# Attention's places in the cycles, loads of a unit one by one, word loads ahead of stores, prologue copies on two engines

## The chip, the core and the metric

The program runs on one core of a Trainium2 chip. The metric is the device time of one execution in microseconds (us); the number for a kernel is the median of its runs. The core has a matrix engine (PE, TensorE), a vector engine (DVE), a scalar engine (ACT), GpSimd (POOL) and a sequencer that mostly asks for transfers (SP). All run beside each other, each takes its own instructions strictly in program order, and they wait for one another through semaphores.

## What is computed

Attention without a score matrix, for 8 batches, 8 heads, 576 positions, 64 columns per head; then two MLPs (512 to 2048 to 512) over all 4608 tokens:

```python
q_s = softmax of q over its 64 columns
k_s = softmax of k over the 576 positions
kv  = einsum('bhsd,bhse->bhde', k_s, v)
x   = einsum('bhsd,bhde->bhse', q_s, kv)          # then (4608, 512)
h = x @ w_in;  x = (h * sigmoid(h)) @ w_out                      # MLP 0
h = x @ w_in2; out = (h * clip(h + 3, 0, 6) / 6) @ w_out2        # MLP 1
```

All inputs are float32; the weights come as 64-bit words, which the kernel turns into float32 on the chip.

## The kernel before

**Cycles.** The tokens are cut into nine tiles of 512: tile t is the first 512 positions of batch t, and tile 8 gathers the 64 positions that each batch has left over (`rest`). The hidden width is cut into eight pairs of 128-column blocks. A cycle g does one MLP m, one tile t and one pair p (`place`, L556), so there are 2 x 9 x 8 = 144 cycles. Cycles 0 to 7 (`first_cycle`, L777) multiply plainly in float32. Cycles 8 to 143 (`cycle`, L687) form the first product of the MLP by a seven-product scheme: `product` (L564) takes one seventh of the tile `ring`, which holds prepared weights, and each operand is split into a high and a low part, so that three matmuls (`mm3`, L72 to L75) stand for one. Two ring buffers take turns, and `load_w` (L264) asks for the ring of cycle g + 2 as soon as cycle g has done its last product. The sum out of PSUM called `s2` (L745) must be done before the seventh product may overwrite its bank B; L750 and L755 are the two sums behind it. `bend` (L579) applies the activation, and `layer_out` (L601, also called G) does the second matmuls one cycle later.

**Ticks.** A cycle has eight places called ticks, `side(0)` to `side(7)`. `run(8 * g + k)` (L683) issues whatever the table `events` holds for that tick. A unit u is one pair of heads of one batch: 32 units. Units 0 to 3 are done in the prologue (L833 to L893), units 4 to 7 in cycles 0 to 7, and the other 24 (`turned`, L275) in cycles 8 to 55, one per two cycles. The loop at L659 gives each unit u a tick x at which its output is formed, and each step a place before it, such as `(-4, at_tsplit)`. So cycles come in two sorts: in one PE forms `kv` of a unit, in the next its output x.

**A unit's steps** (L281 to L496). `at_load` asks for the unit's data: k and the turned q in one tile `kq`, q by rows, and a tile `ev` with k by rows and v. `at_soft` finds the maxima of k (`nm`) and q (`qm`) on DVE and shifts q on GpSimd. `at_sendnm` and `at_send` write such columns to DRAM (`nmd`, `qm`, `qr`), `at_shift` and `at_spread` read them back spread over many partitions (`nb`, `qm`, `qr`). GpSimd then adds (`at_tadd` L330, `at_sub` L382) and multiplies (`at_tmul` L338), ACT takes exponents (`at_texp`, `at_exp`), `at_norm` (L395) forms the reciprocal sums of q on DVE, and `at_tsplit` (L340) splits the turned q into `qh` (ACT) and `ql` (DVE). All these transfers are asked for on SP.

**Weights of MLP 1.** In cycles 56 to about 80 the words of MLP 1 are converted beside the products. `feed` (L84) asks for words into `st` on ACT's queue, `converting` (L114) turns them into `w` (ACT: `magnitude`, L122; DVE: L125 to L140), `operands_w` (L172) forms the seven operands `r`, and `keep` (L203) stores `r` to DRAM, also on ACT's queue. `chain` (L249) strings the jobs of `second` (L231) together, and `pump` (L104) issues their steps by a budget per tick. The weights of MLP 0 go the same way in cycles 0 to 7 (`convert_in`, `convert_out`, L156 to L166).

The order of the instructions on each engine is the order in which this program is written; the framework adds only the waits.

Of the kernel before, what the change touches and what calls it, by code (L numbers as in the profile page):

```python
# [8 lines left out]
F32 = mybir.dt.float32  # L9
# [8 lines left out]
P = 128  # L18
# [17 lines left out]
def attention_two_mlps(ctx: ExitStack, tc: tile.TileContext, kqT, kv5, qn, w1, w2, out):  # L36
# [212 lines left out]
    def chain(jobs, second_mlp=False):  # L249

        out = []
        for k, j in enumerate(jobs):
            if k and len(jobs[k - 1]) < 10:
                out += j[:1]
                j = j[1:]
            elif k:
                out[-1:-1] = j[:1]
                j = j[1:]
            if k and second_mlp and len(jobs[k - 1]) >= 10:
                j = j[:1] + [(0, feed)] + j[1:]  # L260
            out += j
        return out

# [8 lines left out]
    def ahead(u):  # L272
        return u < NP

    def turned(u):  # L275
        return u >= TURNED * NP
# [4 lines left out]
    def at_load(u):  # L281
        b, c = divmod(u, NP)
        s = un[u] = {}
        if ahead(u):
            s["k"] = pro_p.tile([P, S], F32, tag="k", name="k")
            nc.sync.dma_start(out=s["k"], in_=kqT[b, c, :, :S])
        elif turned(u):
            kq = ld_p.tile([P, 2, S], F32, tag="k", name="kq")
            nc.sync.dma_start(out=kq.rearrange("p a s -> p (a s)"), in_=kqT[b, c])
            s["k"], s["t"] = kq[:, 0], kq[:, 1]  # L290
        else:
            s["k"] = ld_p.tile([P, 2, S], F32, tag="k", name="k")[:, 0]
            nc.sync.dma_start(out=s["k"], in_=kqT[b, c, :, :S])
        p = pro_p if ahead(u) else ld_p
        s["q"] = p.tile([QP, 2 * QJ, D], F32, tag="q", name="q")
        nc.sync.dma_start(out=s["q"].rearrange("p j d -> p (j d)"), in_=qn[b, c])
        if ahead(u):
            s["e"] = p.tile([P, 5, P], F32, tag="e", name="e")
            return
        ev = p.tile([P, 2, 5, P], F32, tag="ev", name="ev")  # L300
        s["e"], s["v"] = ev[:, 0], ev[:, 1]
        if turned(u):
            nc.sync.dma_start(out=ev.rearrange("p a j d -> p (a j d)"), in_=kv5[b, c])
        else:
            nc.sync.dma_start(out=s["v"].rearrange("p j d -> p (j d)"), in_=kv5[b, c, :, 5 * P:])

    def at_load_v(u):
        b, c = divmod(u, NP)
# [28 lines left out]
        s = un[u]  # L337
        nc.gpsimd.tensor_tensor(out=s["t"], in0=s["t"], in1=s["qr"], op=ALU.mult)  # L338

    def at_tsplit(u):  # L340
        s = un[u]
        s["qT"] = (
            at_p.tile([P, S], F32R, tag="qh", name="qh"),
            at_p.tile([P, S], F32R, tag="ql", name="ql"),
        )
        split(*s["qT"], s["t"])

    def at_soft(u):
        s = un[u]
# [71 lines left out]
    def at_trq(u, i):  # L421
        s = un[u]
        q = s["q"]
        bq = bank("tq")
        for j in range(3):
            nc.tensor.transpose(
                bq[:, j * QP:(j + 1) * QP],
                q[:, (3 * i + j) * 2:(3 * i + j) * 2 + 2, :].rearrange("p j d -> p (j d)"),
                ident[:QP, :QP],
            )  # L430
        if i == 0:
            if plain(u):
                s["qT"] = at_p.tile([P, S], F32, tag="qh", name="qf")
            else:
                s["qT"] = (
                    at_p.tile([P, S], F32R, tag="qh", name="qh"),
                    at_p.tile([P, S], F32R, tag="ql", name="ql"),
                )
        sl = slice(i * 288, (i + 1) * 288)
        if plain(u):  # L440
            nc.scalar.copy(s["qT"][:, sl], bq[:, :288])
        else:
            qh, ql = s["qT"]
            split(qh[:, sl], ql[:, sl], bq[:, :288])
# [35 lines left out]
    def at_xhalf(u, i):  # L480
        b, c = divmod(u, NP)
        s = un[u]
        bx = bank("x")
        sl = slice(0, HT) if i == 0 else slice(HT, S)
        n = sl.stop - sl.start
        if plain(u):
            nc.tensor.matmul(bx[:, :n], lhsT=s["kv"], rhs=s["qT"][:, sl], start=True, stop=True)
        else:
            (kh, kl), (qh, ql) = s["kv"], s["qT"]
            mm3(bx[:, :n], kh, kl, qh[:, sl], ql[:, sl], True, True)  # L490
        if b == 0:
            nc.scalar.copy(first_x(c)[:, i * HT:(i + 1) * HT], bx[:, :HT])
        else:
            nc.scalar.copy(x_raw(b)[:, c, i * HT:(i + 1) * HT], bx[:, :HT])
        if i:
            nc.scalar.copy(rest[:, c, b * 64:(b + 1) * 64], bx[:, HT:n])  # L496

# [127 lines left out]
    def put(m, t, c, y):  # L625
        if c == 0:
            ys[m, t] = y_p.tile([P, KC, DM], F32, tag="y", name="y")
        o = ys[m, t]
        scale = 0.5 if m == 0 else 1.0
        if c % 2:  # L630
            nc.scalar.activation(out=o[:, c], in_=y, func=AF.Copy, scale=scale)
        else:
            nc.vector.tensor_scalar_mul(o[:, c], y, scale)
        if m and t == NB - 1:
            rows = out.rearrange("(b s) d -> b s d", b=B)[2 * c:2 * c + 2, TB:, :]
            nc.sync.dma_start(out=rows, in_=o[:, c])
# [11 lines left out]
    events = {}  # L648
    m2_p = []
    pre = []  # L650

    def at(tick, fn, *args):
        events.setdefault(tick, []).append((fn, args))
# [4 lines left out]

    for u in range(NP, NU):  # L659
        x = x_at(u)  # L660
        at(x_at(u - 2) - 5 if u - 2 >= NP else -90, at_load, u)
        if turned(u):
            plan = [
                (-28, at_soft), (-27, at_kexp), (-26, at_sendnm), (-26, at_send, "qm"), (-25, at_qexp),
                (-24, at_knorm), (-23, at_norm), (-21, at_shift), (-21, at_spread, "qm"),
                (-20, at_send, "qr"), (-15, at_spread, "qr"), (-14, at_tadd), (-13, at_sub),
                (-10, at_texp), (-9, at_exp), (-8, at_tmul), (-4, at_tsplit),
            ]
        else:
            plan = [  # L670
                (-18, at_soft), (-17, at_kexp), (-16, at_qexp), (-14, at_trk, 0), (-14, at_knorm), (-13, at_norm),
                (-12, at_trk, 1), (-9, at_trq, 0), (-8, at_trq, 1),
            ]
        plan += [(-6, at_kv), (-4, at_kvsplit), (0, at_xhalf, 0), (2, at_xhalf, 1)]
        for d, fn, *args in plan:
            at(x + d, fn, u, *args)
# [100 lines left out]
    def first_cycle(g):  # L777
        A, B_ = banks["A"], banks["B"]

        def side(k):  # L780
            run(8 * g + k)
            pump(FIRST, keep=True)
            if g == NC - 1:
                if k in (2, 3):
                    sums_x(1, k - 2)
                for i in {3: (5,), 4: (1, 6), 5: (2, 3), 6: (7, 4)}.get(k, ()):
                    operand_x(1, i)

        def G(k):
            if g:  # L790
                layer_out(g - 1, k)

        pre = prepare_in(g - 1) if 0 < g < NC - 1 else []
        words_in = convert_in(g + 1) if g + 1 < NC else []
        if g == 1:
            steps.extend(words_in + convert_out(g) + pre)
        else:
            steps.extend(pre[:4] + words_in + pre[4:] + convert_out(g))
# [24 lines left out]
        side(6)  # L823
        G(7)
        side(7)

    with tc.manual_schedule():
# [71 lines left out]
            banks[k] = main_ps.tile([P, TB], F32, tag=k, name=k)  # L899
        for tick in sorted(k for k in events if -90 < k < 0):  # L900
            run(tick)
        for p in range(NC):
            first_cycle(p)
            pump(99)
# [56 lines left out]
```

## Time and profile before

| | |
|---|---|
| median of 3 runs | 1744.61 us (1743.39 to 1744.97) |
| the profiled execution | 1744.62 us, span of its instructions 1742.8 us |
| PE busy | 1655.8 us, 95% of the span |
| DVE, ACT, GpSimd busy | 1034.8 (59%), 739.3 (42%), 182.6 us (10%) |
| moved by DMA | 399.01 MB, mean 229 GB/s |
| granted TensorE clock | 0.988 of full speed |

The span is the time between the first and the last instruction that the profiler saw. A busy share of the whole span is an average over stages with different limits, so the rows below take the stages apart; in the rows by stretch a number in brackets counts instructions, the clock is the granted share of TensorE's full clock, and the DMA column is the mean busy share of the 16 DMA engines. "Idle before" in a row is the time for which that engine did nothing before the instruction, and the arrow names what ended it.

### The profile page before, as it was taken

To read this page: it belongs to the slowest core of one execution; us is meant where nothing else is said; L and a number is where in the kernel's file an instruction comes from. 1 tells how busy PE (TensorE), PEld (TensorE's weight loads), DVE (VectorE), ACT (ScalarE), POOL (GpSimd) and SP (SyncE) were. 2 spreads that over 40 slices of the span, in tenths; PEclk is the share of its full clock that TensorE was granted. 3 is DMA by queue.
4 is the path that set the end of the run, shared out by engine and by line. 5 is a ranking of instruction groups with operands and counts; after the bars stand their busy time and mean duration, and the time that the engine had idled before them with its cause. 6 is when DMAs were issued, how large, how long until landed. Compare 5 with 4: busy or idle time off the path is not lost.

```text
span 1742.8 us, 25018 instructions
## 1 busy us (share of the span) xinstructions
PE 1655.8 (95%) x9816; PEld 1422.0 (82%) x9816; DVE 1034.8 (59%) x1733; ACT 739.3 (42%) x1396; POOL 182.6 (10%) x124
## 2 busy tenths in 40 slices
PE   7899999999999999999999899999999999999994
PEld 4444888888888887898888789999999999999993
DVE  6889677475655657467868674535353535353531
ACT  5444555444443545344545343434343434343431
POOL 2211222231222223200000000000000000000000
PEclk9999999999999999999999999999999999999997
DMA  8568969989998899868887755464655555555540
GB/s 298 189 224 269 259 222 245 234 271 223 239 267 258 235 237 263 226 234 315 328 312 299 305 193 218 169 225 182 230 179 218 192 195 197 202 206 207 197 169 24
DMA packets 71037, 399.01 MB, mean 229 GB/s; under 512 B 20232, under 2 KB 23304, under 8 KB 45320
## 3 DMA queue, kind: packets, MB, share of 16 engines
q1 hardware_dynamic: 66312, 351.27, 63.7%
q10 hardware_dynamic: 4608, 46.14, 6.8%
q8 instruction: 78, 1.28, 0.3%
q14 instruction: 39, 0.32, 0.1%
HBM read 348.91 MB, written 48.47 MB: 228 GB/s over the span
## 4 chain that ended last, share of the span: by engine, by line
PE 70%; DMA 15%; DVE 9%; ACT 2%; issue 1%; POOL 1%; SPq 1%; ACTq 0%; POOLq 0%; DVEq 0%
PE y L73 12%; PE y L74 11%; PE y L75 11%; PE B L73 5%; PE B L74 5%; PE B L75 5%; PE A L73 4%; PE A L74 4%; PE A L75 4%; DMA ring<-wd 4%; DMA qr<-qr 4%; DMA st<-w_dram 3%; DMA q<-qn_dram 2%; PE C L75 2%; PE C L74 2%; PE C L73 2%
## 5 line engine op out<-in xcount | busy, mean ns | idle before, releaser
L70 DVE TENSOR_TENSOR gs<-g,gs 128x512 fp32r<-128x512 f32 x272 | 202.0, 743 | 157.9 <-ACT gs L69 156.4
L73 PE MATMUL B<-o,ring 128*128 128x256 f32 x816 | 234.5, 287 | 30.7 <-DVE s L745 19.9
L69 ACT CAST gs<-g 128x512 fp32r<-128x512 f32 x272 | 168.5, 620 | 207.3 <-DVE g L591 207.0
L73 PE MATMUL A<-op,ring 128*128 128x256 f32 x816 | 231.5, 284 | 10.5 <-DMA ring<-wd 8.6
L74 PE MATMUL A<-op,ring 128*128 128x256 f32 x816 | 230.8, 283 | 1.0 <-DVE op L70 0.9
L75 PE MATMUL B<-o,ring 128*128 128x256 f32 x816 | 231.0, 283 | 0.0
L74 PE MATMUL B<-o,ring 128*128 128x256 f32 x816 | 230.9, 283 | 0.0
L75 PE MATMUL A<-op,ring 128*128 128x256 f32 x816 | 230.8, 283 | 0.0
L73 PE MATMUL y<-woh,gs 128*128 128x512 f32 x576 | 227.8, 395 | 0.0
L74 PE MATMUL y<-wol,gs 128*128 128x512 f32 x576 | 227.7, 395 | 0.0
L75 PE MATMUL y<-woh,gs 128*128 128x512 f32 x576 | 224.5, 390 | 0.0
L73 PEld LDWEIGHTS B<-o,ring 128*128 128x128 f32 x816 | 155.2, 190 | 63.3 <-DVE s L745 29.3
L73 PE MATMUL y<-gs,woh 128*128 128x512 f32 x512 | 205.8, 402 | 0.0
L74 PE MATMUL y<-gs,woh 128*128 128x512 f32 x512 | 203.6, 398 | 0.0
L75 PE MATMUL y<-gs,wol 128*128 128x512 f32 x512 | 201.0, 393 | 0.0
L73 PEld LDWEIGHTS A<-op,ring 128*128 128x128 f32 x816 | 155.9, 191 | 20.6 <-issue 5.0
L74 PEld LDWEIGHTS B<-o,ring 128*128 128x128 f32 x816 | 155.0, 190 | 15.4 <-issue 0.5
L74 PEld LDWEIGHTS A<-op,ring 128*128 128x128 f32 x816 | 155.9, 191 | 6.8 <-DVE op L70 1.4
L75 PEld LDWEIGHTS A<-op,ring 128*128 128x128 f32 x816 | 155.9, 191 | 0.0
L75 PEld LDWEIGHTS B<-o,ring 128*128 128x128 f32 x816 | 155.0, 190 | 0.0
L589 ACT ACTIVATE g<-A,half 128x512 f32<-128x512 f32 x72 | 49.6, 688 | 245.6 <-DVE A L750 245.6
L745 DVE TENSOR_TENSOR s<-B,s 128x256 f32<-128x256 f32 x136 | 57.4, 422 | 158.5 <-PE B L75 156.2
(155 smaller groups left out, 2981.5 us busy)
## 6 DMA issues: line engine op xcount, KB each, us to landing
ring<-wd SPq DMA_DIRECT2D x134, 1792.0 KB, 8.0
st<-w_dram SPq DMA_DIRECT2D x16, 1024.0 KB, 8.3
st<-w_dram ACTq DMA_DIRECT2D x16, 1024.0 KB, 10.6
ev<-kv_dram SPq DMA_DIRECT2D x24, 640.0 KB, 9.8
wd<-ring ACTq DMA_DIRECT2D x8, 1792.0 KB, 9.6
wd<-r ACTq DMA_DIRECT2D x8, 1792.0 KB, 7.6
kq<-kqT_dram SPq DMA_DIRECT2D x24, 576.0 KB, 8.0
q<-qn_dram SPq DMA_DIRECT2D x32, 288.0 KB, 8.5
```

The costliest lines, as they stand in the source:

```text
L69: nc.scalar.copy(hi, src)
L70: nc.vector.tensor_tensor(out=lo, in0=src, in1=f32(hi), op=ALU.subtract)
L73: nc.tensor.matmul(o, lhsT=wh, rhs=xh, start=start, stop=False, **kw)
L74: nc.tensor.matmul(o, lhsT=wh, rhs=xl, start=False, stop=False, **kw)
L75: nc.tensor.matmul(o, lhsT=wl, rhs=xh, start=False, stop=stop, **kw)
L589: nc.scalar.activation(out=a, in_=hb, func=AF.Relu, scale=1.0 / 6.0, bias=half)
L745: nc.vector.tensor_tensor(out=s2, in0=B_[:, lo], in1=s5, op=ALU.add)
```

## The change

1. In a unit of cycles 8 to 55, k, q, `ev` and the turned q (now a tile `t` of its own) are asked for one by one at places of their own; the order on SP changes.
2. The unit's later steps move: `at_tadd`, `at_sub` to tick 0 of a cycle, `at_tmul` from -8 to -4, `at_norm` from -23 to -20, `at_tsplit` is cut into `at_tcast` (ACT) at -3 and `at_tlow` (DVE) at -1. The steps of units 4 to 7 move by one place here and there.
3. In `chain`, the store of a job comes behind the next job's word load.
4. In the first cycles, the `magnitude` of the next weights comes one step earlier in the list.
5. In the prologue, the second half of each PSUM copy goes to DVE.
6. Two of the last four output stores are asked for on ACT's queue.

```diff
@@ chain
             if k and second_mlp and len(jobs[k - 1]) >= 10:
-                j = j[:1] + [(0, feed)] + j[1:]
+                j = j[:1] + [(0, feed), store] + j[1:]
+            if second_mlp and len(jobs[k]) >= 10:
+                store = j[-1]
+                j = j[:-1]
@@ at_load (turned units: kq in one, ev behind it), now at_load, at_load_ev, at_load_t
-            kq = ld_p.tile([P, 2, S], F32, tag="k", name="kq")
-            nc.sync.dma_start(out=kq.rearrange("p a s -> p (a s)"), in_=kqT[b, c])
-            s["k"], s["t"] = kq[:, 0], kq[:, 1]
+        s["k"] = p.tile([P, S], F32, tag="k", name="k")
+        nc.sync.dma_start(out=s["k"], in_=kqT[b, c, :, :S])
...
+    def at_load_t(u):
+        b, c = divmod(u, NP)
+        un[u]["t"] = t = ld_p.tile([P, S], F32, tag="t", name="t")
+        nc.sync.dma_start(out=t, in_=kqT[b, c, :, S:])
@@ at_tsplit
-    def at_tsplit(u):
+    def at_tcast(u):
...
-        split(*s["qT"], s["t"])
+        nc.scalar.copy(s["qT"][0], s["t"])
+
+    def at_tlow(u):
+        s = un[u]
+        nc.vector.tensor_tensor(out=s["qT"][1], in0=s["t"], in1=f32(s["qT"][0]), op=ALU.subtract)
@@ at_trq, at_xhalf
-            nc.scalar.copy(s["qT"][:, sl], bq[:, :288])
+            (nc.vector.tensor_copy if ahead(u) and i else nc.scalar.copy)(s["qT"][:, sl], bq[:, :288])
...
+        copy = nc.vector.tensor_copy if ahead(u) and i else nc.scalar.copy
+        copy((x_raw(b)[:, c] if b else first_x(c))[:, i * HT:(i + 1) * HT], bx[:, :HT])
         if i:
-            nc.scalar.copy(rest[:, c, b * 64:(b + 1) * 64], bx[:, HT:n])
+            copy(rest[:, c, b * 64:(b + 1) * 64], bx[:, HT:n])
@@ put
-            nc.sync.dma_start(out=rows, in_=o[:, c])
+            (nc.scalar if c % 2 else nc.sync).dma_start(out=rows, in_=o[:, c])
@@ the places
-        at(x_at(u - 2) - 5 if u - 2 >= NP else -90, at_load, u)
+        elif turned(u):
+            at(max(x - 42, 0 if turned(u - 2) else before - 11), at_load, u)
+            at(x - 36, at_load_ev, u)
+            at(x - 32, at_load_t, u)
...
-                (-24, at_knorm), (-23, at_norm), (-21, at_shift), (-21, at_spread, "qm"),
-                (-20, at_send, "qr"), (-15, at_spread, "qr"), (-14, at_tadd), (-13, at_sub),
-                (-10, at_texp), (-9, at_exp), (-8, at_tmul), (-4, at_tsplit),
+                (-21, at_shift), (-21, at_spread, "qm"), (-20, at_knorm), (-20, at_norm), (-18, at_send, "qr"),
+                (-12, at_tadd), (-12, at_sub), (-11, at_spread, "qr"), (-10, at_texp), (-9, at_exp),
+                (-4, at_tmul), (-3, at_tcast), (-1, at_tlow),
...
-                (-18, at_soft), (-17, at_kexp), (-16, at_qexp), (-14, at_trk, 0), (-14, at_knorm), (-13, at_norm),
-                (-12, at_trk, 1), (-9, at_trq, 0), (-8, at_trq, 1),
+                (-18, at_soft), (-17, at_kexp), (-15, at_qexp), (-14, at_trk, 0), (-13, at_knorm), (-13, at_norm),
+                (-12, at_trk, 1), (-8, at_trq, 0), (-7, at_trq, 1),
@@ first_cycle (coming holds the jobs whose magnitude is already in the list)
-        words_in = convert_in(g + 1) if g + 1 < NC else []
+        o = convert_out(g)
+        if g + 1 < NC:
+            i = coming.pop()
+            i[-1:-1] = o[:1]
+            if g + 2 < NC:
+                coming.append(convert_in(g + 2))
+                o[-1:-1] = [coming[0].pop(0)]
+            o = o[1:]
```

SP's queue over one unit of cycles 8 to 55, in the kernel before (`nb`, `nmd`, `qm`, `qr` are the columns that go through DRAM, `ring` the prepared weights):

```order
L267 DMA ring<-wd 128x3584
L326 DMA qr<-qr 64x576 x2
L372 DMA nmd<-nm 128x1
L317 DMA qm<-qm 96x2x6
L267 DMA ring<-wd 128x3584
L377 DMA nb<-nmd 128x128
L326 DMA qm<-qm 64x576 x2
L289 DMA kq<-kqT_dram 128x1152
L296 DMA q<-qn_dram 96x768
L303 DMA ev<-kv_dram 128x1280
L317 DMA qr<-qr 96x2x6
```

The same stretch of SP's queue now:

```order
L270 DMA ring<-wd 128x3584
L308 DMA t<-kqT_dram 128x576
L329 DMA qr<-qr 64x576 x2
L379 DMA nmd<-nm 128x1
L320 DMA qm<-qm 96x2x6
L289 DMA k<-kqT_dram 128x576
L291 DMA q<-qn_dram 96x768
L270 DMA ring<-wd 128x3584
L384 DMA nb<-nmd 128x128
L329 DMA qm<-qm 64x576 x2
L301 DMA ev<-kv_dram 128x1280
L320 DMA qr<-qr 96x2x6
```

k and q of a later unit now stand between `nmd` and the second ring, ahead of it; only `ev` stands between the spread of `qm` and the sending of `qr`; `t` comes behind the first ring.

DVE at the start of a cycle that forms a unit's output, in the kernel before (`gs` belongs to the cycle before, `s`, `A` and `B` are the three sums of L745, L750, L755):

```order
L70 TENSOR_TENSOR gs<-g,gs 128x512
L399 TENSOR_REDUCE qs<-q 96x12
L401 TENSOR_SCALAR qs<-qs 96x12
L402 RECIPROCAL qr<-qs 96x12
L460 SCALAR_TENSOR_TENSOR kv<-D,kr,mask 128x128
L70 TENSOR_TENSOR ql<-kq,qh 128x576
L70 TENSOR_TENSOR kl<-kv,kh 128x128
L745 TENSOR_TENSOR s_2852<-B,s_2828 128x256
L750 TENSOR_TENSOR A<-A,s_2852 128x256
L755 TENSOR_TENSOR B<-B,s_2828 128x256
L591 SCALAR_TENSOR_TENSOR g<-g,A 128x512
```

The same place now:

```order
L467 SCALAR_TENSOR_TENSOR kv<-D,kr,mask 128x128
L70 TENSOR_TENSOR kl<-kv,kh 128x128
L399 TENSOR_SCALAR ks<-ks 128x1
L400 RECIPROCAL kr<-ks 128x1
L406 TENSOR_REDUCE qs<-q 96x12
L408 TENSOR_SCALAR qs<-qs 96x12
L409 RECIPROCAL qr<-qs 96x12
L761 TENSOR_TENSOR s_2864<-B,s_2835 128x256
L766 TENSOR_TENSOR A<-A,s_2864 128x256
L771 TENSOR_TENSOR B<-B,s_2835 128x256
L596 SCALAR_TENSOR_TENSOR g<-g,A 128x512
L353 TENSOR_TENSOR ql<-t,qh 128x576
```

`ql` has moved behind the three sums, and the reciprocal sums of q have moved in ahead of them, behind `kl`.

ACT where MLP 1's first `r` is finished, in the kernel before:

```order
L739 COPY s_7161<-C 128x256
L197 CAST r<-st 128x1024
L122 ACTIVATE w<-st 128x1024
L205 DMA wd<-r 128x3584
L96 DMA st<-w_dram 128x2048
L587 ACTIVATE g<-A 128x512
```

And now:

```order
L755 COPY s_7209<-C 128x256
L197 CAST r<-st 128x1024
L122 ACTIVATE w<-st 128x1024
L96 DMA st<-w_dram 128x2048
L205 DMA wd<-r 128x3584
L592 ACTIVATE g<-A 128x512
```

The word load and the store have changed places; so they have at the other seven stores.

## Rows read from the trace of the kernel before

**Rows 1.** Busy time by stretch: us, PE, PEld, DVE, ACT, POOL, clock, DMA, GB/s.

```profile
30.00:164.40 134.40, 122.58 (x350) 58.39 (x350) 116.53 (x158) 57.17 (x96) 26.20 (x13) 0.99 0.66 232
181.70:758.70 577.00, 550.17 (x3406) 484.79 (x3405) 357.54 (x633) 271.78 (x560) 142.89 (x89) 0.99 0.91 241
758.70:1041.10 282.40, 269.83 (x1654) 240.58 (x1653) 215.24 (x342) 134.34 (x225) 0.00 (x0) 0.98 0.76 293
1041.10:1719.30 678.20, 678.20 (x4234) 612.07 (x4232) 312.10 (x545) 246.84 (x450) 0.00 (x0) 1.00 0.53 193
```

**Rows 2.** Timeline of ACT, one copy per cycle (L739): start, us, engine, line.

```profile
181.70 0.37 ACT L739 COPY s<-C 128x256 f32<-128x256 f32 x1 [0.42 <-PE C L75]
...
387.40 0.37 ACT L739 COPY s<-C 128x256 f32<-128x256 f32 x1 [0.28 <-PE C L75]
...
410.78 0.37 ACT L739 COPY s<-C 128x256 f32<-128x256 f32 x1 [0.41 <-PE C L75]
...
758.70 0.37 ACT L739 COPY s<-C 128x256 f32<-128x256 f32 x1 [0.41 <-PE C L75]
...
1041.09 0.36 ACT L739 COPY s<-C 128x256 f32<-128x256 f32 x1
...
1694.47 0.37 ACT L739 COPY s<-C 128x256 f32<-128x256 f32 x1 [0.42 <-PE C L75]
```

**Rows 3.** Waits of PE from 181.7 to 758.7: us in total, times, longest.

```profile
PE B L73 <- DVE s L745: 12.8, 14, 1.9
PE A L73 <- DMA ring<-wd: 8.0, 7, 2.3
PE B L73 <- DVE B L755: 3.7, 2, 2.4
```

**Rows 4.** Waits of SP's queue from 181.7 to 758.7.

```profile
SPq L377 <- DMA nmd<-nm: 152.0, 22, 11.8
SPq L326 <- DMA qr<-qr: 132.1, 23, 9.1
```

**Rows 5.** Timeline of SP's queue, a column sent and read back.

```profile
416.16 0.54 SPq L372 DMA_DIRECT2D nmd<-nm  x1
...
424.85 0.32 SPq L377 DMA_DIRECT2D nb<-nmd  x1
```

**Rows 6.** Busy time by stretch, before and after that column is sent.

```profile
412.00:416.00 4.00, 4.00 (x31) 3.78 (x30) 2.17 (x5) 2.07 (x5) 1.70 (x2) 1.00 1.05 431
418.00:426.00 8.00, 8.00 (x53) 7.14 (x52) 5.50 (x12) 2.55 (x6) 1.43 (x1) 1.00 1.05 59
```

**Rows 7.** Timeline of DVE in the attention stretch.

```profile
527.19 0.76 DVE L70 TENSOR_TENSOR ql<-kq,qh 128x576 fp32r<-128x576 f32 x1 [5.07 <-ACT qh L69]
...
656.91 0.69 DVE L529 TENSOR_TENSOR xr<-xr 128x512 f32<-128x512 f32 x1
657.64 1.82 DVE L529 TENSOR_TENSOR tx<-xr 128x512 f32<-128x512 f32 x1
```

**Rows 8.** Waits of PE from 758.7 to 1041.1.

```profile
PE B L73 <- DVE s L745: 7.2, 3, 5.7
PE B L73 <- DVE B L755: 4.8, 2, 4.0
```

**Rows 9.** Timeline of ACT, a store, a word load and its first reader.

```profile
869.12 0.33 ACTq L205 DMA_DIRECT2D wd<-r  x1
869.53 0.45 ACTq L96 DMA_DIRECT2D st<-w_dram  x1
...
883.99 1.12 ACT L122 ACTIVATE w<-st 128x1024 f32<-128x1024 f32 x1 [5.33 <-DMA st<-w_dram]
```

**Rows 10.** Waits of PE from 30 to 164.4.

```profile
PE D L426 <- POOL q L406: 5.1, 2, 2.7
```

**Rows 11.** Timeline of DVE in the first cycles.

```profile
45.80 0.69 DVE L125 TENSOR_SCALAR wi<-wi 128x1024 f32<-128x1024 f32 x1 [3.48 <-ACT wi L122]
```

**Rows 12.** Busy time by stretch, behind the last matmul.

```profile
1720.00:1741.00 21.00, 0.00 (x0) 0.00 (x0) 0.00 (x0) 0.11 (x1) 0.00 (x0) 0.58 0.13 48
```

More of the change, by code (lines that the diff above doesn't have):

```diff
@@ L283, in at_load @@
         s = un[u] = {}
[L284 to L287, printed above, removed]
-            kq = ld_p.tile([P, 2, S], F32, tag="k", name="kq")
-            nc.sync.dma_start(out=kq.rearrange("p a s -> p (a s)"), in_=kqT[b, c])
-            s["k"], s["t"] = kq[:, 0], kq[:, 1]
-        else:
-            s["k"] = ld_p.tile([P, 2, S], F32, tag="k", name="k")[:, 0]
-            nc.sync.dma_start(out=s["k"], in_=kqT[b, c, :, :S])
         p = pro_p if ahead(u) else ld_p
+        s["k"] = p.tile([P, S], F32, tag="k", name="k")
+        nc.sync.dma_start(out=s["k"], in_=kqT[b, c, :, :S])
         s["q"] = p.tile([QP, 2 * QJ, D], F32, tag="q", name="q")
@@ L298, in at_load, with at_load_ev @@
             s["e"] = p.tile([P, 5, P], F32, tag="e", name="e")
-            return
-        ev = p.tile([P, 2, 5, P], F32, tag="ev", name="ev")
+    def at_load_ev(u):
+        b, c = divmod(u, NP)
+        s = un[u]
+        ev = ld_p.tile([P, 2, 5, P], F32, tag="ev", name="ev")
         s["e"], s["v"] = ev[:, 0], ev[:, 1]
@@ L305, in at_load @@
             nc.sync.dma_start(out=s["v"].rearrange("p j d -> p (j d)"), in_=kv5[b, c, :, 5 * P:])
+    def at_load_t(u):
+        b, c = divmod(u, NP)
+        un[u]["t"] = t = ld_p.tile([P, S], F32, tag="t", name="t")
+        nc.sync.dma_start(out=t, in_=kqT[b, c, :, S:])
     def at_load_v(u):
@@ L345, in at_tsplit @@
         )
-        split(*s["qT"], s["t"])
+        nc.scalar.copy(s["qT"][0], s["t"])
+    def at_tlow(u):
+        s = un[u]
+        nc.vector.tensor_tensor(out=s["qT"][1], in0=s["t"], in1=f32(s["qT"][0]), op=ALU.subtract)
     def at_soft(u):
@@ L490, in at_xhalf @@
             mm3(bx[:, :n], kh, kl, qh[:, sl], ql[:, sl], True, True)
[L491 to L494, printed above, removed]
+        copy = nc.vector.tensor_copy if ahead(u) and i else nc.scalar.copy
+        copy((x_raw(b)[:, c] if b else first_x(c))[:, i * HT:(i + 1) * HT], bx[:, :HT])
         if i:
-            nc.scalar.copy(rest[:, c, b * 64:(b + 1) * 64], bx[:, HT:n])
+            copy(rest[:, c, b * 64:(b + 1) * 64], bx[:, HT:n])
     op_x = {}
@@ L650, in attention_two_mlps @@
     pre = []
+    coming = []
     def at(tick, fn, *args):
@@ L660, in attention_two_mlps @@
         x = x_at(u)
-        at(x_at(u - 2) - 5 if u - 2 >= NP else -90, at_load, u)
+        before = x_at(u - 2) if u - 2 >= NP else None
+        if before is None:
+            at(-90, at_load, u)
+            at(-90, at_load_ev, u)
+        elif turned(u):
+            at(max(x - 42, 0 if turned(u - 2) else before - 11), at_load, u)
+            at(x - 36, at_load_ev, u)
+            at(x - 32, at_load_t, u)
+        else:
+            at(before - 5, at_load, u)
+            at(before - 5, at_load_ev, u)
         if turned(u):
@@ L793, in first_cycle @@
         pre = prepare_in(g - 1) if 0 < g < NC - 1 else []
-        words_in = convert_in(g + 1) if g + 1 < NC else []
+        o = convert_out(g)
[6 more added lines that the diff above has]
+            o = o[1:]
+        else:
+            i = []
         if g == 1:
-            steps.extend(words_in + convert_out(g) + pre)
+            steps.extend(i + o + pre)
         else:
-            steps.extend(pre[:4] + words_in + pre[4:] + convert_out(g))
+            steps.extend(pre[:4] + i + pre[4:] + o)
         ba, bc = bend(g, 0, A), bend(g, 1, B_)
@@ L901, in attention_two_mlps @@
             run(tick)
+        coming.append(convert_in(1))
         for p in range(NC):
```

## Prediction

> **What bounds the kernel now.** I read the busy time by stretch first. From 1041 us to the end PE never stops (678.20 of 678.20 us) [rows 1]; nothing in the change touches that stretch except the last stores. What can move lies before: PE is idle 11.8 us in the first cycles (134.4 - 122.58), 26.8 us in the attention stretch (577.0 - 550.17) and 12.6 us where MLP 1's words are converted (282.4 - 269.83) [rows 1].
>
> Idle time isn't all that a stall costs, so I took the pace of the cycles from one copy that ACT makes in each [rows 2]. Undisturbed, 62 cycles take 1694.47 - 1041.09 = 653.4 us, 10.54 us each. One unit of attention adds work to two cycles; an undisturbed pair takes 410.78 - 387.40 = 23.38 us. So:
> - Attention, 181.70 to 758.70: 46 cycles or 23 pairs in 577.0 us, against 23 x 23.38 = 537.7. **39.3 us are lost.**
> - Conversion, 758.70 to 1041.09: 25 cycles in 282.4 us, against 25 x 10.54 = 263.5. **18.9 us are lost.**
>
> Both are 1.5 times the idle time, because PE's granted clock falls to 0.99 and 0.98 there [rows 1] and work behind a stall runs slower for a while. I use that factor below.
>
> Then the waits of PE. In the attention stretch it waits 12.8 and 3.7 us for two of DVE's sums and 8.0 us for a ring [rows 3]. The sums are late because DVE, which takes its work in order, stands before something else: at 527.19 it had been idle 5.07 us for `qh`, with the sum queued behind [rows 7]. In another place GpSimd works at the same time, and a subtraction of DVE takes 1.82 us where the one before it took 0.69 [rows 7]. In the conversion PE waits 12.0 us for the same two sums [rows 8].
>
> Last the transfers. SP, also in order, stands 152.0 us for `nmd` and 132.1 us for `qr` to land before it may read them back [rows 4]. And `nmd` is dear: it is issued at 416.16, read back at 424.85 [rows 5], and between 418 and 426 the core moves 59 GB/s, with all DMA engines busy, where it moved 431 before [rows 6]. About 8 us of each unit's 23.4 go that way, whatever the order. Over the stretch DMA is 0.91 busy [rows 1], that is 525 us of 577: nearly as much as the 537.7 that PE needs.
>
> **The change part by part.** The sum is against the profiled execution, 1744.62 us (span 1742.8), which is the median to 0.01 us.
>
> *Attention's loads and places.* No work is added but one more request per unit on SP (24 of some 0.5 us, the length of the `nmd` request in [rows 5]; SP has far more time in waits [rows 4]). What goes: `at_soft` no longer stands before a k that was asked for only 9 ticks ahead, now 14; the sums no longer stand behind `qh` and `ql`, since `ql` now follows the three sums, 0.76 us in a place where DVE otherwise waits for ACT; `qr` is asked back seven places behind its sending instead of five, and k and q no longer go between, so SP should stand there little; `nmd` then leaves earlier. What comes: the reciprocal sums of q stand before the sum L745, by my estimate twice a subtraction of that size (0.76 [rows 7]), 1.5 us. I cost them at nothing: DVE is busy 357.54 of 577 us [rows 1], 4 us of each cycle are free, and before that sum it waits for PE; if that cover were gone by half, they would cost 23 x 0.75 = 17 us. Bounds: if nothing is left but PE's pace, -39; if DMA is the true limit, or the cover is gone, about 0. I take two thirds of the sums' 16.5 us as gone, 11 us idle, times 1.5 = **-16**. The last third stays: the cycles at a tile's end, where DVE has seven operand splits to do. The 8.0 us for rings stay, for DMA has less air then.
>
> *Store behind the word load.* At 869.12 ACT asks for a store of 1.8 MB and at 869.53 for the 1 MB of words. They land at 883.99; ACT had then stood 5.33 us [rows 9], DVE behind it, PE behind that. With the words first, they land sooner by what 1.83 MB take: 4.3 us at 431 GB/s [rows 6], and up to twice that where a ring shares the engines; 5.33 lies between. Two of PE's waits are of this kind (up to 5.7 and 4.0 us [rows 8]), and some small ones. About 10 of the 12.0 us go, times 1.5 = 15; the store is later by the words' 2.4 us (1.05 MB at 431 GB/s), up to twice that, and the next job's first operand waits for it on ACT: I take 3 us given back in all. **-12**, between -17 and -6.
>
> *First cycles.* DVE was idle 3.48 us at 45.80 for ACT to make the next magnitude [rows 11], which is now in the queue one step earlier, before the k exponent. The transposes of q, which cost PE 5.1 us of waiting for GpSimd [rows 10], come a place later (about 2 us: 134.4 us are eight cycles of eight places), and what they wait for comes earlier. **-5**, between 0 (DVE, 116.5 of 134.4 us busy [rows 1], has no room) and -10 (most of the 11.8 us).
>
> *Prologue.* Twelve copies of about 0.37 us (so long is one of 128x256 [rows 2]), some 4 us, go from ACT to DVE, which both stand on the way to the first product. Some are side by side now, but DVE also has the first words to convert: **0**, between -2 and +2.
>
> *Last stores.* Behind the last matmul the four stores of 256 KB take 21 us more at 48 GB/s, with a DMA share of 0.13, that is two of sixteen engines [rows 12], however many stores are outstanding. So the engines follow the store's form (its outer size is 2), not its turn, and I take **0**. If ACT's stores went to two other engines, the end would come 11 us sooner. The Trainium skill, "DMA: Bandwidth & Descriptors", section "Issuing engines are not separate DMA queues", says that what SP and ACT ask for runs on the same 16 engines and only issue time is saved; by that the term is 0, and with two queues of their own it would be -11. The trace agrees as to the two engines; ACT's queue is not seen here.
>
> Sum: -16 - 12 - 5 = -33, **1711.6 us**.
>
> **The rivals.**
> - *DMA decides.* With the sums in time, PE asks for rings faster than DMA gives them, and the wait moves from DVE to the ring. For it: 0.91 busy, and the 8 us per unit that no order takes away [rows 1, 6]. Against: SP's 284 us of standing [rows 4] show that DMA was often short of requests rather than of speed. Attention gains nothing, the rest stays: 1744.6 - 17 = 1727.6.
> - *GpSimd is not where its place says.* It starts when its data are there, and a tick holds nothing back. With `qm` and `qr` earlier it may work beside DVE's two-operand subtractions as before [rows 7]. Attention then gains 6: 1721.6.
> - *Slower: the second ring stands behind k and q.* The 0.59 MB of k and q are now asked for just ahead of it, and it had no slack: PE already waits for rings [rows 3]. If `nmd`, and with it the slow stretch, does not leave earlier, each such ring lands 0.59 MB later, 1.4 us at 431 GB/s, times 1.5, times 23 units = +48; with -17 elsewhere and nothing won from DVE: 1775.6. It decides if `nmd` is issued less than 1.4 us earlier in its cycle than now (416.16, which is 5.4 us behind the copy at 410.78).
> - *Nearly all stalls of attention go.* -33 there: 1694.6.
> - *The last stores split over other engines*, beside the forecast: 1700.6.
>
> **How the numbers follow.** Chances: forecast 0.45, DMA decides 0.21, GpSimd unmoved 0.10, slower 0.07, nearly all 0.10, last stores 0.07. The range, 1690 to 1738, takes in all but the slower rival, with the bounds of conversion and first cycles on top of the outer cases. 0.2% is 3.5 us, about what a measurement of this kernel can tell from no change. Slower by more: the rival's 0.07 and 0.01 of others; the same: 0.04, out of "DMA decides" with its other gains at their lower bounds; faster: the rest, 0.88.
>
> **What would show it.** In the conversion no wait of PE for a sum of DVE above 2 us, and 25 cycles in about 270 us. In attention, 23 pairs in about 561 us; SP's waits for `qr` nearly gone; `nmd` issued within 3 us of the cycle's copy; no idle time of DVE before `ql`. In the first cycles the wait for L406 gone. The end from the last matmul to the last instruction as long as before. It is wrong if PE's waits for rings grow above 20 us, if ACT stands before `at_tcast` for GpSimd, or if attention's pairs take longer than 25.1 us.

## The result and the profile after

The changed kernel took 1721.3 us (median of four executions, 1711.2 to 1723.8) against 1744.0 us for the kernel before. The ratio is 0.986, with a 95% interval of 0.982 to 0.991. It is faster, by 23 us in the median. The execution that was profiled is the fastest of the four (1711.23 us, span 1709.4) and 33.4 us below the profiled one of before. The forecast was 1711.6, the range 1690 to 1738.

Busy time by stretch of the kernel after: us, PE, PEld, DVE, ACT, POOL, clock, DMA, GB/s. These are the first cycles, attention, the conversion and the end.

```profile
30.00:165.57 135.57, 126.31 (x377) 62.28 (x376) 122.73 (x168) 60.28 (x104) 26.05 (x13) 0.99 0.69 235
178.29:730.61 552.32, 543.73 (x3407) 483.58 (x3406) 350.47 (x632) 271.15 (x560) 140.52 (x89) 1.00 0.94 252
730.61:1007.56 276.95, 266.71 (x1653) 237.12 (x1652) 214.39 (x342) 133.51 (x225) 0.00 (x0) 1.00 0.78 298
1686.30:1709.40 23.10, 0.00 (x0) 0.00 (x0) 0.00 (x0) 0.60 (x1) 0.00 (x0) 0.56 0.12 45
```

The limits of attention and conversion are ACT's copy of each cycle, which now stands at 178.29, 730.61 and 1007.56; before, it stood at 181.70, 758.70 and 1041.09 [rows 2]. So what lies ahead of attention gave 3.4 us, attention 577.0 - 552.3 = 24.7, the conversion 282.4 - 277.0 = 5.4, and the end nothing: 33.4 us in all by the spans.

Waits of PE in the attention stretch after: us in total, times, longest.

```profile
PE B L73 <- DVE s L761: 5.7, 9, 1.3
PE D L74 <- DVE ql L353: 1.4, 2, 0.8
PE B L73 <- DVE B L771: 0.7, 2, 0.4
PE A L73 <- DMA ring<-wd: 0.4, 1, 0.4
```

The two sums took 16.5 us before [rows 3] and take 6.4 now. The 8.0 us for rings, which the forecast left standing, are down to 0.4. A small wait for the lower part of q is new. On DVE the wait ahead of `ql` (26.9 us in 17 units before) is gone, but DVE now stands 40.8 us in 18 units for ACT's cast `kh` ahead of `kl`, which also comes before the three sums.

Waits of SP's queue in the same stretch.

```profile
SPq L384 <- DMA nmd<-nm: 99.5, 21, 8.6
SPq L329 <- DMA qr<-qr: 51.5, 18, 4.5
```

They were 152.0 and 132.1 [rows 4], so these two waits are 133 us less. Part of that time SP now stands for PE to free a ring buffer (128 us in all, 70 before), so more of these requests come as early as the buffer allows. The ring was asked for more than 8.5 us behind its cycle's copy in 15 of 44 cycles before, and in 2 of 44 now.

Waits of PE in the conversion, for a ring before, then all after.

```profile
PE A L73 <- DMA ring<-wd: 0.5, 1, 0.5
```

```profile
PE A L73 <- DMA ring<-wd: 5.0, 5, 1.8
PE B L73 <- DVE s L761: 2.6, 2, 1.6
PE B L73 <- DVE B L771: 2.5, 2, 1.6
```

The long waits for sums (5.7 and 4.0 us, [rows 8]) are gone, as forecast, but PE now waits for rings, and ACT stands in another place. Its timeline in two cycles there:

```profile
779.29 0.83 ACT L197 CAST r<-w 128x768 fp32r<-128x768 f32 x1 [5.33 <-DMA wd<-r]
...
817.35 0.83 ACT L197 CAST r<-w 128x768 fp32r<-128x768 f32 x1 [5.56 <-DMA wd<-r]
```

ACT no longer waits for words (5.33 us at 883.99, [rows 9]). It waits as long for the store of the previous operand, which has to leave the only buffer `r` before the next may be written.

Waits of PE in the first cycles after.

```profile
PE D L433 <- ACT qf L448: 5.3, 2, 4.8
PE D L433 <- issue: 2.2, 3, 1.0
```

The 5.1 us for GpSimd [rows 10] are gone, and 5.3 us for ACT's copy of the transposed q stand in their place. ACT's timeline, before and after, shows why that copy is late:

```profile
52.76 0.40 ACT L441 COPY qf<-D 128x288 f32<-128x288 f32 x1 [0.96 <-PE D L426]
58.10 1.05 ACT L197 CAST ring<-s 128x1024 fp32r<-128x1024 f32 x1 [4.93 <-DVE s L186]
```

```profile
59.18 1.04 ACT L197 CAST ring<-s 128x1024 fp32r<-128x1024 f32 x1 [6.29 <-DVE s L186]
60.13 0.39 ACT L448 COPY qf<-D 128x288 f32<-128x288 f32 x1
```

The change moved the transposes one place later, and with them the first copy, from ahead of a cast to behind it in ACT's order. That cast waits for DVE, which converts the next words before it makes the cast's sums. It does so in both kernels.

The 3.4 us ahead of attention are two effects of opposite sign. Here is PE at the end of the prologue, before and after, from twelve transposes of q to the first product of cycle 0:

```profile
21.87 1.26 PE L426 MATMUL tq<-ident,q 96*128 96x96 f32 x12
24.24 1.24 PE L487 MATMUL x<-qf,kv 128*128 128x256 f32 x4 [1.11 <-ACT qf L441]
29.97 3.70 PE L577 MATMUL A<-x,wi 128*128 128x512 f32 x8 [0.58 <-ACT rest L496]
```

```profile
21.90 1.26 PE L433 MATMUL tq<-ident,q 96*128 96x96 f32 x12
26.36 0.92 PE L494 MATMUL x<-qf,kv 128*128 128x320 f32 x2 [1.40 <-DVE qf L448]
33.40 3.67 PE L582 MATMUL A<-x,wi 128*128 128x512 f32 x8 [0.79 <-DVE rest L501]
```

The first product comes 11.50 us behind those transposes instead of 8.10. PE waits for the half of the copies that went to DVE, and DVE has them behind the conversion of the first words:

```profile
25.16 0.69 DVE L128 TENSOR_SCALAR wi<-wi 128x1024 uint32<-128x1024 uint32 x1
25.76 0.82 DVE L448 COPY qf<-tq 128x288 f32<-128x288 f32 x2
```

Behind that wait the granted clock is at its lower level (0.50 of full speed, 1.2 GHz). The stretch with the ten matmuls of the last `kv`, before and after, in the form of [rows 1]:

```profile
25.31:26.70 1.39, 1.39 (x11) 1.15 (x9) 1.36 (x2) 0.55 (x3) 0.00 (x0) 1.00 1.00 424
27.10:29.70 2.60, 2.60 (x12) 2.15 (x10) 1.69 (x3) 0.00 (x0) 0.00 (x0) 0.50 0.99 419
```

From the first product to the copy at the start of the attention stretch, the kernel takes 144.9 us in place of 151.7. So the shared copies of the prologue cost 3.4 us, and the stretch behind them gained 6.8.

### The profile page after: what moved, and what is told of

It is laid out like the page before. It is cut to its first block, busy times and chain, and to the rows that moved or that the text cites. A ratio compares the mean times of both kernels' runs of the same rounds, so it can differ in the third digit from the quotient of the medians.

```text
span 1709.4 us, 25068 instructions
## 1 busy us (share of the span) xinstructions
PE 1645.4 (96%) x9816; PEld 1417.9 (83%) x9816; DVE 1031.0 (60%) x1745; ACT 734.5 (43%) x1384; POOL 180.5 (11%) x124
## 4 chain that ended last, share of the span: by engine, by line
PE 68%; DMA 9%; DVE 4%; ACT 2%; issue 1%; ACTq 0%; POOL 0%; SPq 0%; DVEq 0%; POOLq 0%
PE y L73 12%; PE y L74 12%; PE y L75 11%; DMA ring<-wd 6%; PE B L73 5%; PE A L73 5%; PE B L75 5%; PE B L74 5%; PE A L75 5%; PE A L74 4%; DMA wd<-r 2%; PE C L75 2%; PE C L73 2%; PE C L74 2%; DMA qr<-qr 1%
```

## Experiments

All ran on other chips of the same kind, where the kernel before takes 1764 to 1766 us, not 1744. So each is told by its ratio to the kernel before on its own chip.

### The changed kernel again

No edit.

> The changed kernel once more. Its first four executions took 1711.2, 1719.1, 1723.5 and 1723.8 us, and the profiled one is the fastest. Theory 'a wait comes and goes': a second profile near 1721 us has the same cycles as the first but for a few, and about 10 us more in those few, as waits of PE in the attention or conversion stretch. Rival 'clock': the time is spread over all cycles, some 0.6% each, at a lower granted clock, with the same waits. Either way the median is 1718 to 1724.

Measured: 1729.4 us against 1766.4, ratio 0.979 (0.977 to 0.981). The gain is larger here, 37 us. The profiled execution (1733.5 us) against the first profile of the same kernel has the same pace wherever nothing waits (12.07, 11.31 and 10.55 us per cycle). Of the surplus of 22 us, 5.0 lie ahead of attention, 13.9 in attention and 3.4 in the conversion, in single cycles there: one of 15.62 in place of 12.52 us, one of 13.60 in place of 11.38. PE's idle time in attention is 20.5 us in place of 8.6. So waits make most of it; the clock of undisturbed cycles is unchanged. The median lies outside the expected 1718 to 1724, which had not reckoned with the chip.

### Each part alone

Attention's loads and its new places; the rest as before. Of the loads only k and q are asked for earlier, by five ticks for most units; `ev` comes one tick later and the turned q five.

> Only attention's loads and places from the second tile of positions on; the rest as before. In the profile of the change this stretch (46 cycles) took 552.3 us where it took 577.0, so theory 'the places alone do it' expects 1744 - 25 = 1719 us, with ring waits under 2 us. Rival 'the shift against the other stretches counts' (part of the 25 comes from the earlier start of the stretch or from a lucky run): 1725 to 1735.

Measured: 1722.9 us, ratio 0.975 (0.973 to 0.977). This part alone gains 43 us, more than the whole change on the same chip (37). The prologue's shared copies, which it leaves out, cost 3.4 us or more (see the last experiment).

The store of an operand behind the next words:

```
-                j = j[:1] + [(0, feed)] + j[1:]
+                j = j[:1] + [(0, feed), store] + j[1:]
+            if second_mlp and len(jobs[k]) >= 10:
+                store = j[-1]
+                j = j[:-1]
```

> Only the store of a finished word behind the load of the next words. Theory 'the stall moves to the next operand': as in the profile of the change the conversion gains 5 us (7.0 + 4.3 won where the words were late, 6.6 lost where ACT waits for the store to free its buffer), 1739 us, with three such waits of ACT. Rival 'the stall goes' (forecast of the prediction): 12 us, 1732. Rival 'order doesn't matter here, DMA is short of speed': 1744, with words as late as before.

Measured: 1766.1 us, ratio 1.000 (0.997 to 1.002). The theory's 5 us and the rival's 12 us both fall, though the three waits of ACT that the theory named are there. The conversion takes 279.6 us in its profile, and 279.6 in that of the next kernel, which keeps the old order. There ACT stands 10.9 us for words, here 10.5 us for a store, and PE's waits for rings are 6.6 us in place of 0.2: what is won at the words is given back.

The first magnitudes ahead, the places of the first tile's units, the shared copies of the prologue:

> Only the first magnitudes ahead of time, the places of the first tile's units, and the prologue's copies shared. In the profile of the change the first mark of tile 2's second cycle came 3.4 us earlier, so 1740.6 us if that is carried to the end. Rival 'the first cycles are bound by what the words need': 1744. Forecast of the prediction: 1739.

Measured: 1768.5 us, ratio 1.000 (0.999 to 1.002). Forecast and theory both fall, and the rival's time fits, but not its reason: the first product again comes 11.50 us behind the transposes in place of 8.10, so the prologue's copies take back what may be won later. In the first cycles PE waits for ACT's copy as in the changed kernel, and 4.9 us (there 2.2) where the profile shows nothing that it waited for:

```profile
PE D L426 <- ACT qf L441: 5.3, 2, 4.8
PE D L426 <- issue: 4.9, 3, 3.7
```

### Loads or places

Of attention's two edits one each, on the kernel before: first the loads with the old table of places.

> The kernel before, with attention's loads one by one and earlier, and attention's places as before (the split of q's exponents still in one place). Against the kernel before on the same chip, where loads and places together gave 0.975. Theory 'the places': DVE no longer stands for k (39.1 us in the trace of before), but the sums still stand behind the parts of q, so no more than a third of the gain, 0.988 to 0.995. Rival 'the loads': DVE stood for k, so nearly all of it, 0.975 to 0.983.

Measured: 1737.2 us, ratio 0.984 (0.981 to 0.987). Then the places with the old loads:

```
-                (-24, at_knorm), (-23, at_norm), (-21, at_shift), (-21, at_spread, "qm"),
-                (-20, at_send, "qr"), (-15, at_spread, "qr"), (-14, at_tadd), (-13, at_sub),
-                (-10, at_texp), (-9, at_exp), (-8, at_tmul), (-4, at_tsplit),
+                (-21, at_shift), (-21, at_spread, "qm"), (-20, at_knorm), (-20, at_norm), (-18, at_send, "qr"),
+                (-12, at_tadd), (-12, at_sub), (-11, at_spread, "qr"), (-10, at_texp), (-9, at_exp),
+                (-4, at_tmul), (-3, at_tcast), (-1, at_tlow),
```

> The kernel before, with the new places of attention (q's lower parts behind the three sums, q's sums later, its divisors asked back later) and the old loads. Theory 'the places': two thirds of the gain, 0.980 to 0.986, with SP's wait for the divisors down to some 60 us from 132. Rival 'the loads': 0.990 to 1.0. If the two make more together than apart, both come out above 0.985.

Measured: 1759.8 us, ratio 0.996 (0.994 to 0.998). On this chip the loads are worth 28.5 us, the places 6, both together 43. My theory named the wrong one. The traces show what each removes. With the old loads and old places on such a chip (the kernel that moves only the store), waits of SP, DVE and ACT in attention:

```profile
SPq L380 <- DMA nmd<-nm: 190.3, 22, 13.2
SPq L329 <- DMA qr<-qr: 142.2, 23, 10.3
...
DVE nm L355 <- DMA kq<-kqT_dram: 57.4, 15, 6.6
...
ACT qh L69 <- POOL kq L341: 13.1, 3, 6.8
```

With the new places alone:

```profile
SPq L381 <- DMA nmd<-nm: 190.2, 22, 11.9
SPq L326 <- DMA qr<-qr: 135.1, 23, 7.8
...
DVE nm L356 <- DMA kq<-kqT_dram: 63.4, 20, 5.7
...
ACT qh L346 <- POOL kq L338: 37.6, 8, 7.9
```

With the new loads alone:

```profile
SPq L381 <- DMA nmd<-nm: 125.0, 22, 9.7
SPq L326 <- DMA qr<-qr: 40.8, 18, 4.9
```

Here DVE no longer waits for k at all, and SP's two waits fall to half (332.5 to 165.8 us). A ring is asked for more than 8.5 us behind its cycle's copy in 18 of 44 cycles with old loads and places, in 23 of 43 with the places alone and in 7 of 43 with the loads alone. Which of the moved loads does it was not taken apart. The new places leave SP's waits nearly as they were, and ACT stands longer for GpSimd's product (37.6 us in place of 13.1): the product now has its place one tick ahead of ACT's cast instead of four, and its divisors come no earlier. Together the two bring some 9 us more than the sum of both alone (43.5 against 28.5 + 5.8), which is little more than the three intervals leave open (about 7 us).

### The end

Each of the last four stores as two of 64 rows, on attention's loads and places:

```
-            nc.sync.dma_start(out=rows, in_=o[:, c])
+            for h in range(2):
+                nc.sync.dma_start(out=rows[h], in_=o[h * 64:(h + 1) * 64, c])
```

> Attention's loads and places alone (0.975 of before), and each of the four last stores as two of 64 rows. Theory 'a store whose outer size is 2 uses two DMA engines': from the last matmul to the last instruction 8 us in place of 23.3, so 15 us less than attention's loads and places alone, ratio 0.966 to 0.967. Rival 'the tail is the fixed end of a transfer and of the program': 22 to 24 us stay.

Measured: 1708.2 us, ratio 0.968 (0.965 to 0.971), 15 us less than without. Behind the last matmul, as far as the end:

```profile
1702.90:1709.20 6.30, 0.10 (x1) 0.00 (x0) 0.16 (x1) 0.60 (x1) 0.00 (x0) 0.85 0.72 167
```

6.3 us in place of 23.3, at a DMA share of 0.72 in place of 0.12. There are twice as many stores, but six times the share, so here it is the form of the store that sets how many engines it uses. That the change gave two of the four stores to ACT did nothing: from the last matmul to the end it takes 23.5 us, and 23.3 before.

### The order of the stores

Both kernels below stand on the one with halves. First every store behind the load, as in the change:

> Attention's loads and places, the last stores in halves (0.9678 of before, conversion stretch of 25 cycles 279.6 us in its profile), and every store of a finished word behind the load of the next. Theory 'the stall moves': the two late loads of words (5 to 7 us each) go, three waits of ACT for a store come, sum 0 to -5 us: 0.965 to 0.968. Rival 'the stall goes': -12 us, 0.961. Rival 'the order costs the changed kernel its 6.5 us against attention's loads and places alone': 0.971.

Measured: 1707.7 us, ratio 0.968 (0.966 to 0.970), as without the edit. The conversion takes 279.2 us, with ACT's waits:

```profile
ACT r L197 <- DMA wd<-r: 9.9, 3, 4.6
ACT w L122 <- DMA st<-w_dram: 2.3, 1, 2.3
```

Then only those stores behind which no operand is made at once (four of the eight):

```
-                j = j[:1] + [(0, feed)] + j[1:]
+                j = j[:1] + [(0, feed)] + ([store] if len(jobs[k]) < 10 else []) + j[1:]
+            if second_mlp and len(jobs[k]) >= 10 and len(jobs[k + 1]) < 10:
+                store = j[-1]
+                j = j[:-1]
```

> The same, but a store stands behind the next load only where the job that follows has no operand of its own (four stores of eight); where two such jobs follow each other the store goes first as in the kernel before. Theory 'a late store hurts only where the next job needs its buffer at once': no wait of ACT for a store, no late words, the conversion stretch 270 us or less in place of 279.6, ratio 0.962. Rival 'what is left are waits for rings, whatever the order': 277 us or more, 0.966 to 0.968.

Measured: 1701.0 us, ratio 0.964 (0.961 to 0.967). The conversion takes 270.9 us, and PE's waits in it are

```profile
PE A L73 <- DMA ring<-wd: 2.3, 3, 1.3
PE B L73 <- DVE s L763: 1.0, 1, 1.0
```

This is the "about 270 us" of the forecast, but by another edit than the change's. Three profiles with this order (this one and the two kernels below that build on it) show 270.5 to 271.3 us; four with every store behind the load show 277.0 to 280.4, and seven with the old order 277.5 to 284.5. The intervals of the ratios with and without the edit still touch. It is the fastest kernel of the study, 26 us less than the change by the two ratios ((0.979 - 0.964) x 1766).

### Is DMA what is left?

The column of maxima goes over the partitions by one matmul in place of memory, on top of attention's loads and places:

```
+        nc.vector.tensor_copy(nb[:, 0], s["nm"].to_broadcast([P, P]))
...
+        nc.tensor.matmul(b[:, :P], lhsT=nb, rhs=ident, start=True, stop=True)
+        nc.scalar.copy(nb, b[:, :P])
```

> Attention's loads and places alone (0.975 of before), and the column of maxima spread over the partitions by one matmul with the identity, a copy of DVE before and a copy of ACT behind it, in place of its trip through memory (24 sends of 128 numbers of 4 bytes). Theory 'the slow stretch of DMA behind each send makes what is left of attention's stalls': the stretch of 46 cycles goes from 563 to about 548 us, ratio 0.966, and SP's waits for the other sends shrink too. Rival 'DVE at a tile's end makes them': within 4 us of attention's loads and places alone, or later by what the matmuls and copies take (24 x 0.3).

Measured: 1733.3 us, ratio 0.982 (0.979 to 0.985), 10 us more than without it; 4 us of that lie in the first cycles and 6 in the conversion of its profile. The attention stretch of this kernel, and behind it that of attention's loads and places alone:

```profile
181.76:745.36 563.60, 550.94 (x3450) 490.69 (x3449) 357.97 (x653) 276.97 (x581) 137.67 (x89) 1.00 0.74 243
```

```profile
177.64:740.51 562.87, 546.84 (x3406) 486.05 (x3405) 348.12 (x633) 271.92 (x559) 140.72 (x89) 0.99 0.95 247
```

DMA falls from 0.95 to 0.74 busy, SP's 190 us of waits for the two sends are gone, and PE waits for no ring. Yet the stretch takes as long. PE is idle 12.7 us in place of 16.0, but busy 4.1 us longer. So a less busy DMA does not shorten the stretch by itself. Waits of PE, then DVE and POOL at one place:

```profile
PE D L74 <- DVE ql L350: 8.3, 18, 0.9
```

```profile
422.60 1.53 DVE L350 TENSOR_TENSOR ql<-t,qh 128x576 fp32r<-128x576 f32 x1
```

```profile
420.55 1.43 POOL L330 TENSOR_TENSOR t<-t,qm 128x576 f32<-128x576 f32 x1 [8.88 <-DMA qm<-qm]
421.94 1.58 POOL L397 TENSOR_TENSOR ev<-ev,nb 128x640 f32<-128x640 f32 x1
```

GpSimd starts when its data land (420.55, 3.8 us behind the cycle's copy; 9.3 us behind it in the same cycle of the kernel with halves, which keeps the trip through memory). Its second operation ends at 423.52, in the middle of DVE's lower part of q, which takes 1.53 us in place of 0.75. PE waits for that in 18 of the units. Over all units (duration in ns: least, median, most), without the matmul, with it, and in the kernel that follows:

```profile
L350 DVE TENSOR_TENSOR ql<-t,qh x24: 750/752/2003, 171.8 to 735.0; 128x576 fp32r<-128x576 f32 x24
```

```profile
L350 DVE TENSOR_TENSOR ql<-t,qh x24: 750/1463/2077, 175.4 to 739.9; 128x576 fp32r<-128x576 f32 x24
```

```profile
L353 DVE TENSOR_TENSOR ql<-t,qh x24: 751/937/1697, 179.8 to 739.5; 128x576 fp32r<-128x576 f32 x24
```

It takes more than 1 us in 1, 20 and 12 of the 24 units, and each time one or both of these operations of GpSimd run beside it. The Trainium skill, "SBUF — State Buffer", section "SBUF: two separate sides", says that the two share a pair of ports as an exclusive lock, held for a whole instruction, when DVE reads two operands from SBUF; the stretched row agrees. The matmul itself has a price too: an undisturbed cycle with it takes 12.30 us, without it 12.07, so 22 x 0.23 = 5 us.

Then the matmul on the fastest kernel (halves, four stores behind the load), with the maxima of q asked back two places later:

> The last kernel, and the column of maxima by one matmul instead of memory, with the maxima of q asked back two places later, so that GpSimd's addition comes behind DVE's lower part of q. Theory 'GpSimd beside the lower part took back what the shorter transfers gave' (there it took 1.53 us in place of 0.75, and PE waited 8.3 us in 18 units): these waits go, the attention stretch takes 552 to 556 us in place of 563.6, ratio 0.955 to 0.958. Rival 'GpSimd then hits the next two-operand sums of DVE': the waits are found at other sums, 560 us or more, 0.960 to 0.963.

Measured: 1703.9 us, ratio 0.965 (0.964 to 0.967). The waits for the lower part shrink to 2.9 us, others of 3.3 us for DVE's copy come, and the stretch takes 559.2 us, where the same kernel without the matmul takes 558.2. PE is idle 8.8 us in place of 14.1 and busy 6.3 us longer. Neither theory was quite right: the collision is left in half of the units (12 of 24, the third row above), PE waits less for it, and what that freed is about what the matmuls cost.

### Do the first cycles' edits cost anything?

The fastest kernel (halves, four stores behind the load) with the change's prologue and first cycles.

> The kernel with four stores behind the load (0.9641 of before), and the change's edits of the prologue and the first cycles. The changed kernel as a whole came out 6.5 us above attention's loads and places alone; the store's order made no difference, so by subtraction these edits would cost it. Theory 'they cost it': the second mark of tile 2 (end of the first cycles) comes 3 to 6 us later than the 177.6 to 181.8 us of the kernels without them, ratio 0.967 to 0.969. Rival 'they cost nothing, the 6.5 us are how the later stretches fell': mark within 178 to 182 us, ratio 0.963 to 0.965. Forecast of the prediction: 5 us earlier, 0.961.

Measured: 1708.1 us, ratio 0.968 (0.965 to 0.970). The time is that of the theory, but the mark does not show it: it comes at 179.68 us, within the rival's limits (181.77 without the edits), and attention takes 565.6 us in place of 558.2. The intervals of both ratios overlap.

The mark hides what the edits do, for it adds two parts. From the twelve transposes of the prologue to the first product all ten profiles without the edits take 8.09 to 8.11 us, and the four with them 11.50, 11.50, 11.55 and 13.13. So the shared copies cost 3.4 us or more each time. From there to the mark the four take 144.9 to 149.8 us and the ten 145.9 to 153.9: a gain that such a scatter can't prove. In attention the kernels on these chips with the same loads, places and trip through memory take 558.2 to 566.2 us, so 7 us more or less there need no edit. Whether the first cycles' edits pay without the shared copies was not run.

## Why the prediction was right, and where it was not

The sign and the time were right, and attention was the largest part as forecast: the profiled execution gained 33.4 us, the sum was 33. That it fits so well is luck, for the terms miss in both directions, and the profiled execution is the fastest of four; by the medians the gain is 23 us.

- **Attention, -16.** Measured -24.7. The step for the sums held: 10.1 of 16.5 us of waiting went (11 forecast). The factor came out a little lower, 1.35 in place of 1.5 (PE's idle time fell by 18.2 us, from 26.8 to 8.6, and the time by 24.7). What failed is "The 8.0 us for rings stay, for DMA has less air then". With rings asked for on time, 7.6 of the 8.0 us went, times 1.35 = 10 us.
- **Why attention gains.** I gave most of it to the places, the sums "no longer stand behind `qh` and `ql`". The loads carry 28.5 of 43 us, the places alone 6. `qr` was to wait little because it is "asked back seven places behind its sending instead of five"; with these places alone SP waits 135.1 us, nearly as before, with the loads alone 40.8. The other half of that sentence, that k and q no longer go between, fits the loads' part. In the changed kernel SP still stands 51.5 us for `qr`, which is not "nearly gone". DVE's idle time ahead of `ql` (5.07 us once, [rows 7]) is gone, as the forecast asked, but 40.8 us ahead of `kl` have come, before the same sums.
- **Conversion, -12.** Measured -5.4 in the profile, and nothing in the ratio of the edit alone. The mis-sized step is the 3 us "given back in all" by the later store. Three operands stood for their buffer, 11.6 us of ACT's time in all, because the first five operand jobs follow each other and share one buffer, and PE's waits for rings, which had no term, grew from 0.5 to 5.0 us.
- **First cycles, -5.** Measured -6.8 from the first product on, in one profile, a size that the scatter of this stretch does not bear out. The wait for GpSimd went as said, but I did not ask what is late next: ACT's copy of q, which the later place puts behind a cast that waits for DVE.
- **Prologue, 0, between -2 and +2.** Measured +3.4, outside these bounds, and 3.4 to 5.0 in the four profiles with these copies. "DVE also has the first words to convert" was the right thing to ask, but its price was put too low: the copies stand behind those conversions, and PE behind the copies.
- **Last stores, 0.** The end from the last matmul is 23.5 us (23.3 before), with 0.12 of DMA. The Trainium skill, "DMA: Bandwidth & Descriptors", section "Issuing engines are not separate DMA queues", agrees with that; the run with halves shows that the term was the form of the store.
- **The rivals.** "DMA decides" falls: ring waits shrank to 0.4 us while DMA was busier than before (0.94 in place of 0.91). "Slower" needed `nmd` to leave less than 1.4 us earlier; of 22 sends 17 leave within 3 us of their cycle's copy. "GpSimd is not where its place says" was no more than a small part of the change's own time (ACT stands 10.5 us for GpSimd ahead of the cast of q, a sign that I had named against me; it was 5.6 before), but decided the experiment that took memory out of the way.
- **The median.** The forecast took the profiled execution of before, which is its median to 0.01 us, and met the fastest of after; the other three took 8 to 13 us more. No trace of these three exists, so their cause stays open; on another chip the surplus over the first profile was mostly in waits of single cycles.

## What to carry to other kernels

Where an in-order queue both asks for data and waits for its own small sends, split the loads and ask first for what is needed first, and move the places of the arithmetic after that; here the loads alone gave 28.5 us and the places alone 6. Before copies are shared out to a second engine, look at what stands ahead of them in that engine's order: here it cost 3.4 us. When a store is put behind a load, look at when its buffer is written next: move it only where that is not at once. Before weighing who issues the last stores, look at their outer size: 17 us of 23 lay there.

## What was not expected of the hardware

- The same kernel takes 1744 us on one chip and 1764 to 1766 on three others. In the profiles on the first and on one of the others the undisturbed cycles have the same length, but the attention stretch with the old loads and places takes 577.0 and 600.8 us, and SP waits 152.0 and 190.3 us for `nmd`. A gain in waiting thus differs by chip: the change is worth 23 us in the median on the first and 37 on another.
- Taking a slow transfer away (0.95 to 0.74 of DMA's time) gained nothing: GpSimd then started some 5 us earlier in its cycle (9.3 and 3.8 us behind the copy), beside a subtraction of DVE that PE waits for (8.3 us in all), and the matmuls cost about 5 us.
- Behind a wait of 1.40 us in the prologue the granted clock was 0.50 for 2.6 us, and ten matmuls took 1.2 us longer than at 1.00: a short wait on the way to the first product cost nearly twice its length.
